# Splitting a column transform by parity: half the frequencies, sum and difference, and what moves with it

## The chip, the core and the metric

The kernel runs on one core of one Trainium2 chip. The metric is the device time of one execution in microseconds. The profile describes one execution; its span is about 2 us shorter than the device time of the same run. A run lists also the mean granted clock of TensorE, where 1 is full speed. In the profiles PE is TensorE, which does the matmuls and leaves their results in banks of a memory called PSUM; DVE is VectorE, ACT is ScalarE and POOL is GpSimd, which do the element-wise work; SPq is the queue of SyncE, which issues DMA transfers. A tile is 128 rows of the data, a period is the time from one group or tile to the next, and a releaser is the operation that ended a wait.

## The reference

The input is 2048 rows of 576 numbers in bfloat16. A layer norm, a two-dimensional real FFT, a complex weight per frequency, the inverse FFT and a residual add come first; then a second layer norm and a gated feed-forward block with a hidden width of 4608.

```python
def reference(A_x, A_w_r, A_w_i, B_x, B_w_gate, B_w_up, B_w_down):
    def _A_ref(x, w_r, w_i):
        X = rfft2(x); X = X * (w_r + 1j * w_i)
        return irfft2(X, s=(S, D)).astype(bfloat16)
    def _B_ref(x, w_gate, w_up, w_down):
        return (gelu(x @ w_gate) * (x @ w_up)) @ w_down
    h = A_x + _A_ref(_layernorm(A_x), A_w_r, A_w_i)
    return h + _B_ref(_layernorm(h), B_w_gate, B_w_up, B_w_down)     # S, D, F = 2048, 576, 4608
```

## The kernel before

All transforms are matmuls with tables. I call the stages A to D, as the prediction does.

- Stage A: statistics of the first layer norm, and the first half of the transform over rows, into `U`.
- Stage B: for each of 16 groups, the column transform (`st_D`), a small transform and the filter (`st_B`), and the way back (`st_V`). A software pipeline runs `st_D` of group i, `st_B` of i-1 and `st_V` of i-3.
- Stage C: for each of 16 tiles, the inverse column transform (`st_I`), the last small transform with the residual add (`st_N`), and for the first four tiles the second layer norm and a transpose on TensorE (`turn_pe`).
- Stage D: the feed-forward in four blocks of 512 rows. A block has 36 gate/up steps (`gu`), then the down projection. The normalized rows of the next block are transposed by DMA while the block runs.

An operation names what it reads and writes; a helper derives the semaphores.

```python
def st_D(i):                                        # stage B, column transform: 10 matmuls
    for o in range(2):                              # cosine and sine sums
        b = 2 * sl + o
        for dt in range(5):
            P.op(PE, lambda t, ...: t.matmul(bank(b, 0, 128, 0, K2), U[:, dt, g, :, :], FT[:, dt, o, 0:K2], ...))
        # o == 0: VectorE copies to CUS, o == 1: ScalarE copies to CUS
def st_B(i):
    # ... 4 matmuls, YS <- PSUM on ScalarE
    P.op(DVE, ... T1[:, sl, :, :] = YS * WS)        # 580 columns
    # ... T2 in two halves of 290, then on VectorE
    P.op(DVE, ... ZS[.., 0, ..] = T1[.., 0, :] - T1[.., 1, :])
    P.op(DVE, ... ZS[.., 1, ..] = T2[.., 0, :] + T2[.., 1, :])
def st_N(c):                                        # stage C
    for h in range(2):
        b = 4 + h                                   # the same two PSUM banks for every tile
        P.op(PE, lambda t, ...: t.matmul(bank(b, 0, 128, 0, 288), IT[:, c, :], GS[:, sl, 288*h:288*h+288], start=True, stop=True), ...)
    P.op(DVE, ... scalar_tensor_tensor(x2, banks(4, 2, 288), 1.0, x2, op0=mult, op1=add, accum_out=SB2[:, 0, c:c+1]), ...)
    P.op(ACT, ... activation(SQ, XO[:, c, :], Square, accum_out=SB2[:, 1, c:c+1]), ...)
# ... stage D
gu(0)
for tb in range(4):
    for f in range(36):
        gu(36 * tb + f + 1)                         # its first half belongs to step f + 1
        if tb == 0 and f == 20:
            ln2_a(3); ln2_b(3); ln2_c(3)
        if tb < 3 and f % 4 == 3 and f < 16:        # steps 3, 7, 11, 15
            norm(4 * (tb + 1) + f // 4)             # VectorE
            turn_dma(4 * (tb + 1) + f // 4)         # five 128x128 DMA transposes
    for p in range(4):
        down(tb, p)
```

At f = 35 the call `gu(36 * tb + 36)` already contains the first half of the next block's first step, so it needs all the transposed rows of the next block.

Of the kernel before, what the change touches and what calls it, by code (L numbers as in the profile page):

```python
# [10 lines left out]
KW = 290  # L11
ZW = 320
FF = 4608
NT = 16
# [15 lines left out]
def build_tables():  # L30
# [7 lines left out]
    T = {}  # L38
# [20 lines left out]
    T["ITAB"] = I.reshape(128, 16 * 128)  # L59

    d = np.arange(D)[:, None]
    k2 = np.arange(K2)[None, :]
    ph = 2 * np.pi * ((d * k2) % D) / D
    fd = np.zeros((640, 2, KW))
    fd[:D, 0, :K2] = np.cos(ph)
    fd[:D, 1, :K2] = np.sin(ph)
    fd[:, 0, 0] = 0.0
    T["FTAB"] = fd.reshape(5, 128, 2 * KW).transpose(1, 0, 2).reshape(128, -1)

    B = np.zeros((2, 3, 16, 4, 2, 128))  # L70
# [40 lines left out]
    T["BTAB"] = B.reshape(2, 3, 128, 128).transpose(2, 0, 1, 3).reshape(128, -1)  # L111
# [3 lines left out]
    dc = np.arange(D)[None, :]  # L115
# [6 lines left out]
    dt_ = np.zeros((5, 128, D))  # L122
    dt_[0], dt_[1] = C[0:128], N[0:128]
    dt_[2], dt_[3] = C[128:256], N[128:256]
    dt_[4, 0:33] = C[256:289]
    dt_[4, 64:96] = N[256:288]
    T["EYE"] = np.eye(128)
    T["DTAB"] = dt_.transpose(1, 0, 2).reshape(128, -1)
# [156 lines left out]
def _build(nc, A_x, A_w_r, A_w_i, B_w_gate, B_w_up, B_w_down, out):  # L285
# [34 lines left out]
    FT = sb.alloc("FT", [128, 5, 2, KW], BF16)  # L320
    BT = sb.alloc("BT", [128, 2, 3, 128], BF16)
# [13 lines left out]
    DT = sb.alloc("DT", [128, 5, D], BF16)  # L335
    IT = sb.alloc("IT", [128, NT, 128], BF16)
    GS = sb.alloc("GS", [128, 2, D], BF16)
# [22 lines left out]
    P.op(POOL, lambda g: g.memset(WS[:, :, :, K2:KW], 0.0), w=["Wz"])  # L360
    P.op(POOL, lambda g: g.memset(U[64:128, 4, :, :, :], 0.0), w=["Uz"])
    xv = A_x[0].rearrange("(p c) d -> p c d", c=NT)
    ov = out[0].rearrange("(p c) d -> p c d", c=NT)
    for i, (c0, c1) in enumerate(((0, 2), (2, 4), (4, 8), (8, 12), (12, 16))):
        P.dma(SP, XO[:, c0:c1, :], xv[:, c0:c1, :], f"x{i}", w=[("X", c) for c in range(c0, c1)])
# [5 lines left out]
    def w_loads(pl, hf, eng):  # L371
        g0, g1 = ((1, 9), (9, 16))[hf]
        src = (A_w_r, A_w_i)[pl]
        o = []
        for jj in range(4):
            o.append((WS[jj:64:4, g0:g1, pl, 0:K2], (16 * jj + g0) * K2, [[128 * K2, 16], [K2, g1 - g0], [1, K2]], jj))
            o.append((WS[64 + jj:128:4, g0:g1, pl, 0:K2], (64 + 16 * jj + 16 - g0) * K2, [[128 * K2, 16], [-K2, g1 - g0], [1, K2]], 4 + jj))
        if hf:
            for p0 in range(2):
                o.append((WS[64 * p0:64 * p0 + 64, 0, pl, 0:K2], 64 * p0 * K2, [[128 * K2, 16], [16 * K2, 4], [1, K2]], 8 + p0))  # L380
        return [lambda d=d, off=off, ap=ap, h=h: P.dma(eng, d, bass.AP(src.tensor, off, ap), f"w{pl}{hf}", r=["Wz"], w=[("W", hf, pl, h)]) for d, off, ap, h in o]

    for f in w_loads(0, 0, SP) + w_loads(0, 1, SP):
        f()
# [3 lines left out]
    P.dma(SP, IT[:, :, :].rearrange("p a b -> p (a b)"), dram["ITAB"][:, :], "it", w=["IT"])  # L388
    P.dma(SP, IDT[:, :], dram["EYE"][:, :], "eye", w=["IDT"])

    P.op(POOL, lambda g: g.memset(YS[:, :, :, K2:KW], 0.0), w=["Yz"])
    P.op(POOL, lambda g: g.memset(ZS[:, :, :, K2:ZW], 0.0), w=["Zz"])
    for f in w_loads(1, 0, POOL):
        f()
    wrest = w_loads(1, 1, POOL)


    def ln1_act(q):
        c = 4 * q + 3
        P.op(ACT, lambda a, c=c: a.activation(JNK[:, 0, :], XO[:, c, :], ACTF.Identity, accum_out=SA[:, 0, c:c + 1]),  # L400
             r=[("X", c)], w=[("SA0", c), "J0"])
        P.op(ACT, lambda a, c=c: a.activation(JNK[:, 1, :], XO[:, c, :], ACTF.Square, accum_out=SA[:, 1, c:c + 1]),  # L402
             r=[("X", c)], w=[("SA1", c), "J1"])
# [5 lines left out]
    def ln1_var(q):  # L409
        for c in range(4 * q, 4 * q + 3):  # L410
            P.op(DVE, lambda v, c=c: v.bn_aggr(MV1[:, c, :], ST1[:, c, :, :]), r=[("ST1", c, 0), ("ST1", c, 1)], w=[("MV1", c)])
        c = 4 * q + 3
        P.op(DVE, lambda v, c=c: v.scalar_tensor_tensor(TM[:, 0, c:c + 1], SA[:, 0, c:c + 1], 1.0 / (D * D), SA[:, 0, c:c + 1],
                                                        op0=ALU.mult, op1=ALU.mult), r=[("SA0", c)], w=[("TM", c)])
        P.op(DVE, lambda v, c=c: v.scalar_tensor_tensor(MV1[:, c, 1:2], SA[:, 1, c:c + 1], 1.0 / D, TM[:, 0, c:c + 1],
                                                        op0=ALU.mult, op1=ALU.subtract), r=[("SA1", c), ("TM", c)], w=[("MV1", c)])

    def ln1_sqrt(q):
        cs = slice(4 * q, 4 * q + 4)
        P.op(ACT, lambda a, cs=cs: a.activation(RS1[:, cs], MV1[:, cs, 1], ACTF.Sqrt, bias=EPT[:, 0:1]),  # L420
             r=[("MV1", c) for c in range(4 * q, 4 * q + 4)] + ["EPT"], w=[("SD1", q)])

    def ln1_scale(q, eng):
        cs = slice(4 * q, 4 * q + 4)
        P.op(DVE, lambda v, cs=cs: v.reciprocal(RS1[:, cs], RS1[:, cs]), r=[("SD1", q)], w=[("RS1", q)])
        if eng == POOL:
            P.op(POOL, lambda g, cs=cs: g.tensor_tensor(ATS[:, cs, :], ATB[:, cs, :], RS1[:, cs].unsqueeze(2).to_broadcast([128, 4, 128]), op=ALU.mult),
                 r=[("RS1", q), "ATB"], w=[("ATS", c) for c in range(4 * q, 4 * q + 4)])
        else:
            for c in range(4 * q, 4 * q + 4):  # L430
                P.op(DVE, lambda v, c=c: v.tensor_scalar(ATS[:, c, :], ATB[:, c, :], RS1[:, c:c + 1], None, op0=ALU.mult),
                     r=[("RS1", q), "ATB"], w=[("ATS", c)])
# [5 lines left out]
    def a_mm(q, dt):  # L438
        b = (5 * q + dt) % 7
        w = 128 if dt < 4 else 64  # L440
        for i in range(4):
            c = 4 * q + i
            P.op(PE, lambda t, b=b, w=w, i=i, c=c, dt=dt: t.matmul(bank(b, 0, w, 128 * i, 128 * i + 128), XO[:, c, 128 * dt:128 * dt + w],
                                                                  ATS[:, c, :], start=True, stop=True),
                 r=[("X", c), ("ATS", c)], w=[("PS", b)])

    def a_ev(q, dt, eng):
        b = (5 * q + dt) % 7
        w = 128 if dt < 4 else 64
        src = bank(b, 0, w).rearrange("p (n g e) -> p n g e", n=4, g=16)  # L450
        dst = U[0:w, dt, :, 4 * q:4 * q + 4, :].rearrange("p g n e -> p n g e")
        if eng == DVE:
            P.op(DVE, lambda v, s=src, d=dst: v.tensor_copy(d, s), r=[("PS", b)], w=[("U", q, dt)])
        else:
            P.op(ACT, lambda a, s=src, d=dst: a.activation(d, s, ACTF.Copy), r=[("PS", b)], w=[("U", q, dt)])  # L455

    P.op(ACT, lambda a: a.activation(SA[:, 0, 0:1], EPT[:, 0:1], ACTF.Sqrt), r=["EPT"], w=[("SA0", 0)])
    ln1_act(0)
    ln1_act(1)
    idle_mm(24)  # L460
    for c in range(3):
        ln1_tile(c)
    ln1_var(0)
    ln1_sqrt(0)
    ln1_act(2)
    ln1_tile(4)
    ln1_scale(0, POOL)
    for f in wrest[:4]:
        f()
    ln1_tile(5)  # L470
    ln1_tile(6)
    ln1_var(1)
    a_mm(0, 0)
    a_ev(0, 0, ACT)
    ln1_sqrt(1)
    for dt in range(1, 5):
        a_mm(0, dt)
    a_ev(0, 1, ACT)
    a_ev(0, 2, ACT)
    ln1_tile(8)  # L480
    ln1_scale(1, POOL)
    for f in wrest[4:7]:
        f()
    ln1_tile(9)
    ln1_tile(10)
    ln1_var(2)
    a_ev(0, 3, ACT)
    a_ev(0, 4, ACT)
    ln1_sqrt(2)
    ln1_act(3)  # L490
    idle_mm(4)
    for dt in range(5):
        a_mm(1, dt)
        a_ev(1, dt, ACT)
    ln1_tile(12)
    ln1_scale(2, POOL)
    for f in wrest[7:]:
        f()
    ln1_tile(13)
    ln1_tile(14)  # L500
    ln1_var(3)
    ln1_sqrt(3)
    idle_mm(4)
    for dt in range(5):
        a_mm(2, dt)
    a_ev(2, 0, ACT)
    a_ev(2, 1, DVE)
    ln1_scale(3, DVE)
    a_ev(2, 2, ACT)
    a_ev(2, 3, DVE)  # L510
    a_ev(2, 4, ACT)
    idle_mm(4)
    for dt in range(5):
        a_mm(3, dt)
        a_ev(3, dt, (ACT, DVE)[dt % 2])
    idle_mm(3)


    ukeys = [("U", q, dt) for q in range(4) for dt in range(5)] + ["Uz"]

    def st_D(i):
        g = GORD[i]
        sl = i % 2
        for o in range(2):
            b = 2 * sl + o
            for dt in range(5):
                P.op(PE, lambda t, b=b, o=o, dt=dt, g=g: t.matmul(bank(b, 0, 128, 0, K2), U[:, dt, g, :, :], FT[:, dt, o, 0:K2],  # L527
                                                                 start=(dt == 0), stop=(dt == 4)),
                     r=ukeys + ["FT"], w=[("PS", b)])
            if o == 0:  # L530
                P.op(DVE, lambda v, b=b, sl=sl: v.tensor_copy(CUS[:, sl, 0, 0:K2], bank(b, 0, 128, 0, K2)), r=[("PS", b)], w=[("CU", sl)])
            else:
                P.op(ACT, lambda a, b=b, sl=sl: a.activation(CUS[:, sl, 1, 0:K2], bank(b, 0, 128, 0, K2), ACTF.Copy), r=[("PS", b)], w=[("SU", sl)])  # L533

    def st_B(i):
# [3 lines left out]
        for b, tabs in ((4, (0, 1)), (5, (1, 2))):  # L539
            for o in range(2):  # L540
# [238 lines left out]
```

## Time and profile before

The median was 518.59 us (518.15 to 519.65, 4 runs). The profiled span was 516.4 us.

| stage | from, us | to, us | length, us |
|---|---|---|---|
| A | 0 | 21.80 | 21.8 |
| B | 21.80 | 64.16 | 42.4 |
| C | 64.16 | 89.56 | 25.4 |
| D | 89.56 | 516.4 | 426.8 |

A stage begins with its first matmul. First, from the page of the kernel before, the head of the chain that ended last: shares of the span by engine.

```profile
PE 93%; DVE 2%; ACT 2%; DMA 2%; issue 0%; SPq 0%; DVEq 0%
```

Next, the same chain in order of time. The columns are start in us, length in us, and engine, output and line. L527 is the column transform, L541 the small transform, L560 and L564 the way back; L699 is gate/up and L720 is down.

```profile
31.87 1.34 PE PS L527 x10
33.21 0.50 PE PS L541 x4
33.71 0.44 PE PS L560 x4
34.15 0.24 PE PS L564 x4
34.38 1.34 PE PS L527 x10
...
92.03 70.04 PE PS L699 x648
162.06 35.39 PE PS L720 x288
```

One group of stage B lasts 34.38 - 31.87 = 2.51 us, and all of it is TensorE. In stage D the block 0 sequence is 70.04 us of gate/up followed at once by 35.39 us of down: no wait. The 648 matmuls of this piece are 36 steps of 18, so one step takes 1.946 us.

The timeline of the kernel before in stage C (start, length, engine, line, operation, operands; in brackets the idle time before and its releaser):

```profile
68.08 0.41 PE L611 MATMUL PS<-GS,IT 128*128 128x288 bf16 x2
...
68.53 0.76 DVE L614 SCALAR_TENSOR_TENSOR XO<-PS,XO 128x576 bf16<-128x576 f32 x1 [0.70 <-PE PS L611]
...
69.55 0.41 PE L611 MATMUL PS<-GS,IT 128*128 128x288 bf16 x2
```

The residual add (L614) takes 0.76 us and reads the PSUM banks that the next tile's pair of matmuls (L611) overwrites. It is done at 69.29, before the matmuls would start at 69.55. The tile period is 1.47 us.

Last, the normalization of step 15 of block 0, in the timeline of VectorE:

```profile
123.96 0.64 DVE L640 TENSOR_SCALAR HN<-XO,TM,RS_59 128x576 bf16<-128x576 bf16 x2
```

its five transposes, in the timeline of the SyncE queue:

```profile
124.62 6.19 SPq L193 DMA_TRANSPOSE HT_84<-HN  x5
```

and the end of the traffic, in a table of windows (the length of the window, the busy time of PE, of its weight loads PEld, of DVE, ACT and POOL with counts, then the granted clock, the DMA share and GB/s):

```profile
131.75:132.00 0.25, 0.25 (x6) 0.13 (x4) 0.06 (x1) 0.05 (x1) 0.00 (x0) 1.00 0.00 0
```

The five transposes occupy the queue for 6.19 us, and the DMA engines are quiet from about 131.75. So a normalization leads to transposed rows about 7.8 us later. In this kernel nothing waits for them.

### The profile page before, as it was taken

What the parts mean: (1) busy time and instruction counts of PE and PEld (TensorE: products, weight loads), DVE (VectorE), ACT (ScalarE), POOL (GpSimd) and SP (SyncE); (2) the same over time, 40 slices, a digit from 0 to 9 for tenths busy, and PEclk for the clock granted to TensorE, in tenths of its full rate; (3) what the DMA queues carried; (4) which work ended last, traced back from release to release, by engine and by line L of the source; (5) the groups of instructions that cost most, each with busy time, mean ns of one, the idle gap of its engine ahead of it and who ended that gap; (6) DMA issues with size and microseconds to landing.
All of it is one profiled execution on the core that took longest, in us unless ns stands there. A gap on an engine that the chain in (4) does not pass through costs nothing.

```text
span 516.4 us, 10131 instructions
## 1 busy us (share of the span) xinstructions
PE 507.4 (98%) x4425; PEld 295.9 (57%) x4427; DVE 184.5 (36%) x428; ACT 152.7 (30%) x285; POOL 27.8 (5%) x48
## 2 busy tenths in 40 slices
PE   8899899999999999999999999999999999999997
PEld 3577577444445775444457754444477644444776
DVE  5687758344432112443321124433311133333111
ACT  5756677423521002332320013323200033233000
POOL 8800130000000000000000000000000000000000
PEclk9999999999999999999999999999999999999999
DMA  8999791011000000110000000100000000000000
GB/s 289 289 343 307 208 361 44 4 24 22 7 1 2 18 18 11 22 22 11 1 1 18 18 11 20 22 15 1 1 13 18 18 1 1 0 2 1 13 18 17
DMA packets 23899, 28.64 MB, mean 55 GB/s; under 512 B 11408, under 2 KB 17680, under 8 KB 23856
## 3 DMA queue, kind: packets, MB, share of 16 engines
q1 hardware_dynamic: 20560, 15.68, 10.9%
q0 software_dynamic: 3152, 11.80, 7.0%
q8 instruction: 34, 0.56, 0.5%
q10 hardware_dynamic: 144, 0.52, 0.3%
q14 instruction: 9, 0.07, 0.0%
HBM read 23.67 MB, written 2.36 MB: 50 GB/s over the span
## 4 chain that ended last, share of the span: by engine, by line
PE 93%; DVE 2%; ACT 2%; DMA 2%; issue 0%; SPq 0%; DVEq 0%
PE PS L699 55%; PE PS L720 27%; PE PS L527 4%; PE PS L602 3%; DMA XO<-in_A_x_dram 2%; PE PS L541 1%; ACT U L455 1%; PE PS L560 1%; PE PS L611 1%; PE PS L564 1%; DVE XO L614 0%; ACT JNK L400 0%; DVE ST_53 L407 0%; ACT JNK L402 0%; ACT YS L544 0%
## 5 line engine op out<-in xcount | busy, mean ns | idle before, releaser
L711 ACT ACTIVATE GL<-PS 128x512 bf16<-128x512 f32 x144 | 85.8, 597 | 293.9 <-PE PS L699 293.1
L712 DVE TENSOR_TENSOR AT<-GL,PS 128x512 bf16<-128x512 bf16 x144 | 98.9, 688 | 174.3 <-PE PS L699 169.8
L699 PE MATMUL PS<-HT_69,WGU 64*128 64x512 bf16 x1296 | 144.4, 376 | 0.0
L699 PE MATMUL PS<-HT_84,WGU 64*128 64x512 bf16 x1296 | 144.4, 376 | 0.0
L720 PE MATMUL PS<-WD,AT 128*128 128x288 bf16 x1152 | 141.8, 286 | 0.0
L720 PEld LDWEIGHTS PS<-WD,AT 128*128 128x128 bf16 x1152 | 112.4, 98 | 29.9 <-issue 1.7
L699 PEld LDWEIGHTS PS<-HT_84,WGU 64*128 64x128 bf16 x1296 | 64.5, 94 | 77.9 <-issue 0.5
L699 PEld LDWEIGHTS PS<-HT_69,WGU 64*128 64x128 bf16 x1296 | 64.5, 94 | 76.8 <-issue 0.7
L723 DVE TENSOR_TENSOR OS<-PS,XO 128x288 bf16<-128x288 f32 x32 | 14.6, 458 | 126.0 <-PE PS L720 126.0
L602 PE MATMUL PS<-DT,V 128*128 128x288 bf16 x160 | 22.1, 286 | 0.5 <-ACT V L567 0.5
L527 PE MATMUL PS<-FT,U 128*128 128x289 bf16 x160 | 22.3, 287 | 0.2 <-ACT U L455 0.2
L602 PEld LDWEIGHTS PS<-DT,V 128*128 128x128 bf16 x160 | 15.4, 98 | 4.3 <-issue 0.6
L527 PEld LDWEIGHTS PS<-FT,U 128*128 128x128 bf16 x160 | 14.5, 97 | 5.1 <-issue 0.4
L614 DVE SCALAR_TENSOR_TENSOR XO<-PS,XO 128x576 bf16<-128x576 f32 x16 | 12.1, 756 | 9.6 <-PE PS L611 9.3
L436 PE MATMUL PS<-ZD 128*128 128x512 bf16 x37 | 11.8, 475 | 1.5 <-POOL ZD L358 1.3
L617 ACT ACTIVATE SQ<-XO 128x576 bf16<-128x576 bf16 x16 | 10.9, 682 | 5.0 <-DVE XO L614 4.8
L407 DVE BATCH_NORM_STATS2 ST_53<-XO 128x6 f32<-128x288 bf16 x24 | 9.2, 443 | 5.7 <-DMA XO<-in_A_x_dram 5.7
L544 ACT ACTIVATE YS<-PS 128x578 bf16<-128x578 f32 x16 | 10.5, 655 | 1.8 <-PE PS L541 0.7
L604 ACT ACTIVATE GS<-PS 128x576 bf16<-128x576 f32 x16 | 10.2, 635 | 2.6 <-PE PS L602 2.6
L541 PE MATMUL PS<-CUS,BT 128*128 128x289 bf16 x64 | 10.6, 286 | 0.2
L533 ACT ACTIVATE CUS<-PS 128x289 bf16<-128x289 f32 x16 | 6.6, 413 | 14.0 <-PE PS L527 14.0
L546 DVE TENSOR_TENSOR T_79<-YS,WS 128x580 bf16<-128x580 bf16 x16 | 7.3, 459 | 9.1 <-ACT YS L544 9.1
(57 smaller groups left out, 173.2 us busy)
## 6 DMA issues: line engine op xcount, KB each, us to landing
WD<-in_B_w_down_dram POOLq DMA_DIRECT2D x9, 576.0 KB, 9.3
WGU<-in_B_w_gate_dram POOLq DMA_DIRECT2D x4, 1152.0 KB, 17.7
WGU<-in_B_w_up_dram SPq DMA_DIRECT2D x4, 1152.0 KB, 22.5
out_dram<-OS SPq DMA_DIRECT2D x32, 72.0 KB, 1.6
XO<-in_A_x_dram SPq DMA_DIRECT2D x3, 576.0 KB, 8.2
FT<-c_ftab SPq DMA_DIRECT2D x1, 725.0 KB, 12.7
DT<-c_dtab SPq DMA_DIRECT2D x1, 720.0 KB, 14.6
HT_84<-HN SPq DMA_TRANSPOSE x40, 2.4
```

The costliest lines, as they stand in the source:

```text
L436: P.op(PE, lambda t: t.matmul(bank(7), ZD[:, 0:128], ZD[:, :], start=True, stop=True), r=["ZD"], w=[("PS", 7)])
L527: P.op(PE, lambda t, b=b, o=o, dt=dt, g=g: t.matmul(bank(b, 0, 128, 0, K2), U[:, dt, g, :, :], FT[:, dt, o, 0:K2], start=(dt == 0), stop=( ...
L541: P.op(PE, lambda t, b=b, o=o, tb=tabs[o], sl=sl, sp_=sp_: t.matmul(bank(b, 0, 128, 0, K2), BT[:, sp_, tb, :], CUS[:, sl, o, 0:K2], start= ...
L544: P.op(ACT, lambda a, sl=sl: a.activation(YS[:, sl, :, 0:K2], banks(4, 2, K2), ACTF.Copy), r=[("PS", 4), ("PS", 5)], w=[("Y", sl)])
L602: P.op(PE, lambda t, b=b, h=h, kt=kt, c=c: t.matmul(bank(b, 0, 128, 0, 288), V[:, kt, c, :, :], DT[:, kt, 288 * h:288 * h + 288], start=(k ...
L614: P.op(DVE, lambda v, x2=x2, c=c: v.scalar_tensor_tensor(x2, banks(4, 2, 288), 1.0, x2, op0=ALU.mult, op1=ALU.add, accum_out=SB2[:, 0, c:c ...
L617: P.op(ACT, lambda a, sl=sl, c=c: a.activation(SQ[:, sl, :], XO[:, c, :], ACTF.Square, accum_out=SB2[:, 1, c:c + 1]), r=[("X", c)], w=[("S ...
L699: op = P.op(PE, lambda t, h0=h0, kt=kt, wt=wt, f=f, b=b, HT=HT, s=(half == 0 and j in (0, 5)), e=(half == 1 and j in (3, 8)): t.matmul(ban ...
L711: P.op(ACT, lambda a, s2=s2, b0=b0: a.activation(GL[:, s2, :], bank(b0), ACTF.Gelu_apprx_tanh), r=[("PS", b0)], w=[("GL", s2)])
L712: P.op(DVE, lambda v, s2=s2, b0=b0, f=f: v.tensor_tensor(AT[:, f, :], GL[:, s2, :], bank(b0 + 1), op=ALU.mult), r=[("GL", s2), ("PS", b0 + ...
L720: P.op(PE, lambda t, b=b, h=h, f=f, p=p: t.matmul(bank(b, 0, 128, 0, 288), AT[:, f, 128 * p:128 * p + 128], WD[:, f, 288 * h:288 * h + 288 ...
L723: P.op(DVE, lambda v, b=b, h=h, p=p, c=c: v.tensor_tensor(OS[:, p % 2, 288 * h:288 * h + 288], bank(b, 0, 128, 0, 288), XO[:, c, 288 * h:2 ...
```

## The change

For the cosine and sine sums over d, the frequencies k and 288-k differ only in the sign of the odd d (for the sines also in the sign of the whole, which the table of the small transform takes up). So the even and the odd d are summed for 145 frequencies, and VectorE makes the sum and the difference. That is 6 matmuls of 290 columns instead of 10 of 289 per group; the inverse likewise computes half the columns, with 6 + 4 matmuls per tile instead of 10 + 2. The small transform `st_B` gets six matmuls instead of four, with the same number of columns in all. The diff, cut to its core:

```diff
 def st_D(i):
-            for dt in range(5):
-                P.op(PE, ... matmul(bank(b, 0, 128, 0, K2), U[:, dt, g, :, :], FT[:, dt, o, 0:K2], ...))
-            # copies of the two sums, one on DVE and one on ACT
+            for dt in range(3):
+                us = (2 * o + dt) if dt < 2 else 4
+                P.op(PE, ... matmul(bank(b, 0, 128, 0, 2 * HK), U[:, us, g, :, :], FT[:, o, dt, :], ...))
+        P.op(ACT, ... ES = even sums, fp32)
+        P.op(DVE, ... CUS[.., 0:HK] = e2 + o2)
+        P.op(DVE, ... CUS[.., K2 - 1:HK - 1:-1] = e2 - o2)
 def st_B(i):
-        # T2 in two halves; both Z sums on DVE
+        P.op(DVE, ... T2[:, sl, :, :] = YS * WS[:, g, 1::-1, :])
+        P.op(POOL, ... ZS[:, z3, 0, 0:KW] = T1[:, sl, 0, :] - T1[:, sl, 1, :])
+        P.op(POOL, ... ZS[:, z3, 1, 0:KW] = T2[:, sl, 0, :] + T2[:, sl, 1, :])
 def st_N(c):
+            for i in range(2):        # 4 matmuls instead of 2, into the same banks 4 and 5
-        P.op(ACT, ... Square ...)
+        if c < 4:
+            square(c, SQ[:, sl, :], ("SQ", sl))
 # stage D
-            if tb == 0 and f == 20:
-                ln2_a(3); ln2_b(3); ln2_c(3)
-            if tb < 3 and f % 4 == 3 and f < 16:
-                norm(4 * (tb + 1) + f // 4)
-                turn_dma(4 * (tb + 1) + f // 4)
+            if tb == 0 and f < 12:
+                square(4 + f, OS[:, f % 2, :], ("OS", f % 2, 0))
+            if tb == 0 and f == 14:
+                ln2_a(1); ln2_b(1); ln2_c(1)
+            if tb < 3 and f % 4 == 3 and 16 <= f < 32:
+                norm(4 * (tb + 1) + f // 4 - 4)
+                turn_dma(4 * (tb + 1) + f // 4 - 4)
# ... also changed: stage A works in six groups (2, 2, 4, 4, 2, 2 tiles) with fewer idle matmuls,
# ... all filter loads go through the SyncE queue, and the copy of turned tiles moves from DVE to ACT
```

Three things travel with the idea. The Z sums go to GpSimd. Twelve of the sixteen squares for the second layer norm are deferred to block 0 of the feed-forward. The statistics of these twelve tiles are then ready only after step 14 of block 0, and normalization and transposes come at steps 19, 23, 27 and 31, in all blocks.

## The prediction

> **What bounds it now.** The chain of waits gives TensorE 93% of the 516.4 us span. Read in time order it has four stages. A (layer norm, first transform) ends at 21.8. B (column transform, filter, group transform) runs 21.8 to 64.2 in a steady 2.51 us per group, TensorE without a gap (1.34 column matmuls, 0.50, 0.44, 0.24). C (inverse) runs 64.2 to 89.6, 1.47 us per tile (1.23 + 0.24), dense but for the layer-norm turns. D (feed-forward) is 70.04 + 35.39 us, four times, with no gap at all.
>
> **What the change does.**
> 1. Stage B: 6 column matmuls of 290 columns for 10 of 289. At 0.134 us each that is 0.54 us less per group; TensorE's own period falls to about 2.03 (six shorter matmuls replace four, same columns). But the two Z sums move from VectorE to GpSimd. The 128x512 GpSimd multiply took 1.03-1.05 us, so 128x290 should take about 0.6 (estimate), two 1.2. The Trainium skill (SBUF — State Buffer, "Who interferes with whom") says a VectorE op with two SBUF inputs and a GpSimd op that reads SBUF exclude each other for the whole instruction. T1 and T2 are such ops (0.37 us spacing each). Serial: 0.37+0.46+1.2 plus hand-overs = about 2.15 us, more than TensorE's 2.03. So the period should be 2.15-2.25. The drain gets longer by about 0.7 us (GpSimd sums slower than VectorE's 0.22). Stage B gains about 4 us rather than the 8.6 of the matmul count.
> 2. Stage A: smaller groups, but the same bn_stats and ScalarE evictions, and the last statistics now wait on ScalarE sums in the middle. I expect 0 to 2 us longer, +0.8.
> 3. Stage C: 6+4 matmuls instead of 10+2 save 0.24 per tile by count. But the 0.76 us residual add reads the single pair of PSUM banks and has only 0.74 us of matmuls to hide behind (before 1.23). Period about 0.48+0.76+0.1 = 1.36 us, not 1.23. Gain about 2.2 us. Deferring ScalarE squares helps little there.
> 4. Stage D: the squares (0.87 us of ScalarE, twelve times) fit beside 0.60 us GELUs in a 1.946 us step, with no extra table load. But normalization and DMA transposes move from steps 3,7,11,15 to 19,23,27,31. In before, step 15's normalization began at 123.96; its five transposes occupied the queue until 130.81 and DMA activity ended about 131.8, i.e. 8.7 us after the matmuls of that step's eviction ended (123.09). In after, the first matmul of the next token block is only 3 steps = 5.84 us away. TensorE should stall about 2.9 us at the end of blocks 0, 1 and 2: +8.7 us.
>
> **Sum.** 518.5 + 0.8 - 4 - 2.2 + 8.7 = 521.8; leaning slightly to the gains, 521.0 us, range 514.5 to 527. Chances: faster by over 2% 0.05, within 2% 0.88, slower by over 2% 0.07.
>
> **What would show each step.** Stage B period 2.15-2.25 with GpSimd sums and T1/T2 not overlapping, TensorE waiting on GpSimd or ScalarE (1); 2.03 refutes the exclusion. Stage C period near 1.36, TensorE waiting on the residual add before the inverse group matmuls (3). Three TensorE gaps of about 3 us in the feed-forward, just before the block's last gate/up step, released by the transposes' DMA (4). Granted clock staying near 1.
>
> **What would make it wrong.** The transposes landing sooner, so no stall (then near 512); the exclusion weaker than stated (2 us faster) or GpSimd sums over 0.7 us (slower); filter loads, now all on one queue, landing late; the clock dropping after the 3 us gaps (slower).

## The result, and the profile after

The changed kernel took 532.04 us (median of 4 runs, 530.35 to 532.78); the ratio is 1.0252, with a 95% interval of 1.0223 to 1.0281. The change is slower by 2.5%, and the prediction of 521.0 us with a range to 527 missed it. The mean granted clock of its four runs was 0.974 to 0.987; that of the kernel before was 0.999 in its profiled run.

The profiled spans are 531.0 and 516.4 us. Where the 14.6 us lie:

| stage | before, us | after, us | measured | predicted |
|---|---|---|---|---|
| A | 21.80 | 22.94 | +1.1 | +0.8 |
| B | 42.36 | 38.27 | -4.1 | -4 |
| C | 25.40 | 26.13 | +0.7 | -2.2 |
| D | 426.84 | 443.66 | +16.8 | +8.7 |

The page of the changed kernel, head of the chain:

```profile
PE 85%; DVE 8%; issue 3%; ACT 1%; POOL 1%; DMA 1%; DVEq 0%; POOLq 0%
```

and the chain in order of time through stage D (L721 is gate/up, L742 is down):

```profile
90.05 68.10 PE PS L721 x630
158.15 3.83 issue
161.98 2.96 PE PS L721 x18
164.94 36.18 PE PS L742 x288
...
269.21 3.01 issue
272.22 3.80 PE PS L721 x18
...
379.51 3.05 issue
382.56 4.02 PE PS L721 x18
386.58 36.29 PE PS L742 x288
```

The three waits add to 9.9 us. They are labelled "issue": the profile saw no releaser for them, so the label alone does not say what was waited for. The time goes on after the waits. The 18 matmuls of the step that follows take 2.96, 3.80 and 4.02 us instead of 1.946, and two of the three down projections take 36.18 and 36.29 instead of 35.39. Together that is 4.9 + 1.7 = 6.6 us of slow matmuls. (The first wait is the longest because one of its five transposes held the queue for 2.06 us instead of 1.23; why it did stays open.) The windows around the first wait show the reason:

```profile
158.00:162.00 4.00, 0.17 (x4) 0.05 (x4) 0.69 (x1) 0.00 (x0) 0.00 (x0) 1.00 0.12 25
...
163.50:164.00 0.50, 0.50 (x6) 0.26 (x4) 0.00 (x0) 0.22 (x1) 0.00 (x0) 0.50 0.00 0
...
166.50:167.00 0.50, 0.50 (x5) 0.40 (x4) 0.00 (x0) 0.00 (x0) 0.00 (x0) 0.97 0.00 0
```

In each line the third number from the end is the granted clock. It stays at 1 through the wait and for about a microsecond after it, falls to 0.50 at 163.12, and is back at 166.53, 3.41 us later.

The timeline of stage C, to be held against that of before (L633 are the four small matmuls, L636 the residual add):

```profile
67.31 0.65 PE L633 MATMUL PS<-GS,IT 128*128 128x288 bf16 x4 [0.20 <-DVE XO L636]
...
68.00 0.76 DVE L636 SCALAR_TENSOR_TENSOR XO<-PS,XO 128x576 bf16<-128x576 f32 x1 [0.84 <-PE PS L633]
...
68.92 0.65 PE L633 MATMUL PS<-GS,IT 128*128 128x288 bf16 x4 [0.20 <-DVE XO L636]
```

The tile period is 68.92 - 67.31 = 1.61 us, longer than the 1.47 before although there are fewer matmuls. The matmuls wait 0.20 us for the residual add of the tile before.

Stage B in the timeline of TensorE:

```profile
37.05 0.92 PE L540 MATMUL PS<-FT,U 128*128 128x290 bf16 x6
37.81 0.67 PE L557 MATMUL PS<-CUS,BT 128*128 128x289 bf16 x6
38.32 0.60 PE L575 MATMUL PS<-VT,ZS 128*128 128x256 bf16 x4
38.85 0.31 PE L579 MATMUL PS<-VT,ZS 128*64 128x128 bf16 x4
39.09 0.30 PE L540 MATMUL PS<-FT,U 128*128 128x290 bf16 x1
```

One group now takes 39.09 - 37.05 = 2.04 us, without a gap on TensorE. The groups of VectorE and GpSimd operations (busy time in us, mean ns of one, then idle time before and its releaser) are, before,

```profile
L546 DVE TENSOR_TENSOR T_79<-YS,WS 128x580 bf16<-128x580 bf16 x16 | 7.3, 459 | 9.1 <-ACT YS L544 9.1
```

and after, where L562 is T1 and L565 and L566 the Z sums:

```profile
L565 POOL TENSOR_TENSOR ZS<-T_80 128x290 bf16<-128x290 bf16 x16 | 12.7, 792 | 13.4 <-DVE T_80 L562 13.0
...
L566 POOL TENSOR_TENSOR ZS<-T_81 128x290 bf16<-128x290 bf16 x16 | 11.4, 711 | 2.3
L562 DVE TENSOR_TENSOR T_80<-YS,WS 128x580 bf16<-128x580 bf16 x16 | 11.3, 704 | 1.2 <-ACT YS L560 1.1
```

T1, the same operation as before, has gone from 459 to 704 ns.

### The profile page after: what moved, and what is told of

Same layout as the page of the kernel before. It is cut to its first block, busy times and chain, and to the rows that moved or that the text cites. A ratio compares the mean times of both kernels' runs of the same rounds, so it can differ in the third digit from the quotient of the medians.

```text
span 531.0 us, 10050 instructions
## 1 busy us (share of the span) xinstructions
PE 504.2 (95%) x4346; PEld 289.1 (54%) x4347; DVE 183.7 (35%) x387; ACT 155.5 (29%) x296; POOL 43.3 (8%) x64
## 4 chain that ended last, share of the span: by engine, by line
PE 85%; DVE 8%; issue 3%; ACT 1%; POOL 1%; DMA 1%; DVEq 0%; POOLq 0%
PE PS L721 54%; PE PS L742 27%; PE PS L633 2%; DVE T_80 L562 2%; DVE XO L636 1%; PE PS L618 1%; DVE ST_53 L418 1%; DMA XO<-in_A_x_dram 1%; DVE CUS L546 1%; DVE CUS L547 1%; ACT U L476 1%; POOL ZS L566 1%; DVE V L584 1%; POOL ZS L565 1%; PE PS L540 1%
## 5 line engine op out<-in xcount | busy, mean ns | idle before, releaser
L721 PE MATMUL PS<-HT_85,WGU 64*128 64x512 bf16 x1296 | 149.0, 380 | 6.9 <-issue 6.9
L721 PE MATMUL PS<-HT_69,WGU 64*128 64x512 bf16 x1296 | 149.2, 380 | 3.0 <-issue 3.0
L742 PE MATMUL PS<-WD,AT 128*128 128x288 bf16 x1152 | 143.5, 288 | 0.0
L742 PEld LDWEIGHTS PS<-WD,AT 128*128 128x128 bf16 x1152 | 113.1, 99 | 32.0 <-issue 2.8
L721 PEld LDWEIGHTS PS<-HT_85,WGU 64*128 64x128 bf16 x1296 | 65.2, 95 | 86.3 <-issue 10.5
L721 PEld LDWEIGHTS PS<-HT_69,WGU 64*128 64x128 bf16 x1296 | 65.5, 95 | 80.5 <-issue 6.1
L745 DVE TENSOR_TENSOR OS<-PS,XO 128x288 bf16<-128x288 f32 x32 | 14.6, 457 | 127.7 <-PE PS L742 127.7
L636 DVE SCALAR_TENSOR_TENSOR XO<-PS,XO 128x576 bf16<-128x576 f32 x16 | 12.1, 757 | 14.6 <-PE PS L633 14.5
L540 PE MATMUL PS<-FT,U 128*128 128x290 bf16 x96 | 15.8, 305 | 0.9 <-DVE U L474 0.9
L618 PE MATMUL PS<-DT,V 128*128 128x289 bf16 x96 | 15.8, 306 | 0.5 <-ACT V L582 0.5
L565 POOL TENSOR_TENSOR ZS<-T_80 128x290 bf16<-128x290 bf16 x16 | 12.7, 792 | 13.4 <-DVE T_80 L562 13.0
L463 PE MATMUL PS<-ATS,XO 128*128 128x128 bf16 (+1 forms) x80 | 6.4, 222 | 6.4 <-POOL ATS L442 6.2
L633 PE MATMUL PS<-GS,IT 128*128 128x288 bf16 x64 | 10.5, 285 | 2.0 <-DVE XO L636 1.6
L620 ACT ACTIVATE GS<-PS 128x578 bf16<-128x578 f32 x16 | 10.4, 648 | 5.5 <-PE PS L618 5.3
L557 PE MATMUL PS<-CUS,BT 128*128 128x289 bf16 (+2 forms) x96 | 11.2, 254 | 0.6 <-ACT ES L543 0.4
L562 DVE TENSOR_TENSOR T_80<-YS,WS 128x580 bf16<-128x580 bf16 x16 | 11.3, 704 | 1.2 <-ACT YS L560 1.1
L618 PEld LDWEIGHTS PS<-DT,V 128*128 128x128 bf16 x96 | 9.7, 103 | 3.6 <-issue 0.6
L566 POOL TENSOR_TENSOR ZS<-T_81 128x290 bf16<-128x290 bf16 x16 | 11.4, 711 | 2.3
L575 PE MATMUL PS<-VT,ZS 128*128 128x256 bf16 x64 | 9.6, 272 | 2.1 <-POOL ZS L566 2.1
```

Source lines behind the costliest of these rows:

```text
L540: P.op(PE, lambda t, b=b, o=o, dt=dt, us=us, g=g: t.matmul(bank(b, 0, 128, 0, 2 * HK), U[:, us, g, :, :], FT[:, o, dt, :], start=(dt == 0) ...
L562: P.op(DVE, lambda v, g=g, sl=sl: v.tensor_tensor(T1[:, sl, :, :], YS[:, sl, :, :], WS[:, g, :, :], op=ALU.mult), r=[("Y", sl)] + wk, w=[( ...
L565: P.op(POOL, lambda v, sl=sl, z3=z3: v.tensor_tensor(ZS[:, z3, 0, 0:KW], T1[:, sl, 0, :], T1[:, sl, 1, :], op=ALU.subtract), r=[("T1", sl) ...
L566: P.op(POOL, lambda v, sl=sl, z3=z3: v.tensor_tensor(ZS[:, z3, 1, 0:KW], T2[:, sl, 0, :], T2[:, sl, 1, :], op=ALU.add), r=[("T2", sl)], w= ...
L618: P.op(PE, lambda t, b=b, h=h, i=i, kt=kt, c=c: t.matmul(bank(b, 0, 128, 0, K2), V[:, kt, c, :, :], DT[:, 3 * h + i, 0:K2], start=(i == 0) ...
L633: P.op(PE, lambda t, b=b, h=h, i=i, c=c, rhs=rhs: t.matmul(bank(b, 0, 128, 0, 288), IT[:, h * i, c, :], rhs, start=(i == 0), stop=(i == 1) ...
```

## The experiments

My theory after reading the result had two parts. The late transposes alone make the waits of stage D; and the waits lower TensorE's clock, which costs another 6.6 us. The rivals were that the deferred squares are to blame, and that the clock falls for some other reason. Eleven kernels ran. Those of one group ran on one chip, with its own runs of the kernel before. e1 and e7 are the changed kernel with one edit, and e3 is the kernel before with one. All others contain the edit of e2 as well; only what they add is shown.

| run | median, us | ratio to before (95%) | mean clock, profiled run | B, us | C, us | D, us |
|---|---|---|---|---|---|---|
| changed kernel | 532.04 | 1.0252 (1.0223-1.0281) | 0.981 | 38.3 | 26.1 | 443.7 |
| e1_dense_gap | 526.19 | 1.0133 (1.0103-1.0163) | 0.993 | 37.6 | 25.7 | 438.3 |
| e2_early | 516.02 | 0.9935 (0.9907-0.9963) | 0.989 | 38.4 | 25.7 | 427.1 |
| e3_before_late | 531.24 | 1.0230 (1.0192-1.0268) | 0.996 | 42.4 | 25.4 | 438.7 |
| e4_early_nbuf | 514.84 | 0.9914 (0.9889-0.9939) | 0.990 | 37.2 | 25.2 | 427.1 |
| e5_z_dve | 515.98 | 0.9943 (0.9919-0.9966) | 0.997 | 37.9 | 26.4 | 427.1 |
| e6_warm | 513.96 | 0.9906 (0.9883-0.9929) | 1.000 | 37.1 | 25.0 | 427.1 |
| e7_step18 | 519.91 | 1.0016 (0.9988-1.0044) | 0.997 | 37.1 | 25.0 | 431.6 |
| e8_squares_in_c | 515.46 | 0.9936 (0.9900-0.9972) | 0.990 | 37.3 | 26.7 | 427.1 |
| e9_z_split | 513.70 | 0.9903 (0.9873-0.9933) | 1.000 | 35.9 | 25.0 | 427.1 |
| e10_turn_later | 513.17 | 0.9888 (0.9863-0.9913) | 0.990 | 37.4 | 23.8 | 427.1 |
| e11_all | 511.43 | 0.9856 (0.9832-0.9881) | 1.000 | 36.7 | 23.0 | 427.1 |

All outputs were correct. The kernel before had medians of 519.38 (e1 to e4), 518.35 (e5 to e8) and 518.71 us (e9 to e11).

### e1_dense_gap: the same waits, with TensorE kept busy

```diff
+            if f == 35 and tb < 3:
+                for _ in range((17, 14, 14)[tb]):     # useless, into a free PSUM bank
+                    P.op(PE, lambda t, tb=tb: t.matmul(bank(7), WGU[:, 0, 0:128], HTS[tb % 2][:, 0, :], ...), w=[("PS", 7)])
             gu(36 * tb + f + 1)
```

> The changed kernel, with 17, 14 and 14 useless 512-column matmuls put into a free PSUM bank just before the first step of blocks 1, 2 and 3, where TensorE waits 3.8, 3.0 and 3.1 us. Theory (idleness lowers the clock): the useless work takes what was idle time, about 3 us each, the wait itself costs the same, but the granted clock stays at 1 and the 6.6 us of slow matmuls after the three waits vanish: about 525.5 us. Rival (the clock falls for another reason, such as load): the clock still falls to about 0.5 after the waits and the time stays near 532 us.

Measured: 526.19 us, 5.9 us below the changed kernel; its slowest run (527.59) lies below the fastest of the changed kernel (530.35). In the windows of this run, of which the first covers the end of block 0's steps and the useless matmuls, and the others the first step of the next block and the down projection:

```profile
157.00:161.00 4.00, 3.87 (x20) 1.69 (x22) 0.69 (x1) 0.00 (x0) 0.00 (x0) 1.00 0.08 16
161.00:163.00 2.00, 2.00 (x21) 0.81 (x18) 0.09 (x1) 0.60 (x1) 0.00 (x0) 1.00 0.00 0
163.00:165.00 2.00, 2.00 (x19) 1.61 (x17) 0.60 (x1) 0.00 (x0) 0.00 (x0) 1.00 0.00 0
```

The clock stays at 1.00 after all three waits, and the first steps take 2.05, 2.05 and 2.12 us. The waiting itself is still there (stage D 438.3 us). So it is the idleness of TensorE in these waits that lowers the clock after them.

### e2_early: normalization and transposes back to an earlier place

```diff
-            if tb < 3 and f % 4 == 3 and 16 <= f < 32:
-                norm(4 * (tb + 1) + f // 4 - 4)
-                turn_dma(4 * (tb + 1) + f // 4 - 4)
+            f0 = 15 if tb == 0 else 3
+            if tb < 3 and f % 4 == 3 and f0 <= f < f0 + 16:
+                norm(4 * (tb + 1) + (f - f0) // 4)
+                turn_dma(4 * (tb + 1) + (f - f0) // 4)
```

> The changed kernel with normalization and transposes moved back: steps 15, 19, 23, 27 in block 0 (after the deferred statistics at step 14) and steps 3, 7, 11, 15 in blocks 1 and 2. Theory (the late transposes alone make the feed-forward longer): no wait of TensorE in the feed-forward, granted clock 1 there, the whole 16.5 us back: about 515.5 us, 3 us below the kernel before. Rival (the twelve deferred squares on ScalarE, or the extra matmuls elsewhere, share the blame): a gain of less than 14 us.

Measured: 516.02 us, as the theory had it. The chain of this run in stage D:

```profile
89.82 70.04 PE PS L721 x648
159.86 35.38 PE PS L742 x288
```

There is no wait, and stage D is back at 427.1 us. The twelve deferred squares are still in block 0 of this kernel, so they cost TensorE nothing there.

### e3_before_late: only the late place, in the kernel before

```diff
-            if tb < 3 and f % 4 == 3 and f < 16:
-                norm(4 * (tb + 1) + f // 4)
-                turn_dma(4 * (tb + 1) + f // 4)
+            if tb < 3 and f % 4 == 3 and 16 <= f < 32:
+                norm(4 * (tb + 1) + f // 4 - 4)
+                turn_dma(4 * (tb + 1) + f // 4 - 4)
```

> The kernel before with only normalization and transposes moved to steps 19, 23, 27, 31 of each block, as the change has it; nothing else of the change. Theory: three waits of about 3 us with the clock falling to half after each, together 15 to 17 us: about 534.5 us. Rival (the waits need the deferred squares or the new DMA order as well): under 525 us.

Measured: 531.24 us (529.59 to 533.17). The place alone costs 2.3%, nearly as much as the whole change. The size was below the expected 534.5, and the chain of the profiled run shows why (L699 is gate/up):

```profile
160.17 2.98 issue
163.15 3.60 PE PS L699 x18
...
270.22 3.82 issue
274.04 2.12 PE PS L699 x18
...
379.64 3.04 issue
382.68 2.12 PE PS L699 x18
```

All three waits are there, with 9.8 us in all, but only the first was followed by a slow step. The mean clock of the four runs went from 0.996 to 0.987, and the slower runs are those with the lower clock. A wait of 3 to 4 us thus lowers the clock often but not always. It is not the length alone: the second wait, 3.82 us, did not, and the first, 2.98 us, did. What decided is worked out in the section on why the prediction was wrong.

### e7_step18: one step earlier

```diff
-            if tb < 3 and f % 4 == 3 and 16 <= f < 32:
+            if tb < 3 and f % 4 == 2 and 16 <= f < 32:
```

> The changed kernel with normalization and transposes just one step (1.95 us) earlier, steps 18, 22, 26, 30. Theory: the waits shrink by 1.95 us each, from 3.8, 3.0, 3.1 to about 1.9, 1.1, 1.1 us, 4.1 us in all, and gaps this short leave the clock at 1: early transposes plus 4.1, about 520 us, a gain of 12 us although only 5.9 us of waiting went. If the clock falls after such short gaps too, 523 to 526 us.

Measured: 519.91 us (518.35 to 520.41). The waits in the profiled run added to 3.9 us, the longest being 1.7, and the clock was 1.00 after each. So 1.95 us less of waiting per block gained 12 us. The profiled run was the fastest of the four; the others were 1.4 to 2.1 us slower, with mean clocks of 0.987 to 0.990, and no trace says where their clock fell.

### e4_early_nbuf: a second pair of banks in stage C

```diff
-            b = 4 + h
+            b = (4 if c % 2 == 0 else 6) + h      # and the residual add reads the same pair
```

> As the run with early transposes, and the inverse group matmuls of odd tiles go to PSUM banks 6 and 7 instead of 4 and 5, so that a tile no longer waits for the residual add of the tile before it. Theory (that single pair of banks makes the 1.60 us period of the inverse stage): period about 1.25 us, stage from 26.2 to about 22.5 us, time about 3.5 us below the run with early transposes, so about 512 us. Rival (ScalarE's evictions or VectorE's own work set the period): under 1 us gained.

Measured: 514.84 us, 1.2 us below the run with early transposes, where 3.5 was expected. The timeline of TensorE in this run:

```profile
64.36 0.65 PE L633 MATMUL PS<-GS,IT 128*128 128x288 bf16 x4
...
65.99 0.67 PE L633 MATMUL PS<-GS,IT 128*128 128x288 bf16 x4 [0.22 <-ACT GS L620]
...
67.24 0.66 PE L633 MATMUL PS<-GS,IT 128*128 128x288 bf16 x4
```

The period is now 1.63 and 1.25 us in turn, and the longer one waits for ScalarE's copy. Stage C is 0.5 us shorter than in the run with early transposes; of the 1.5 us between the two profiled spans 1.1 lie in stage B, which this edit does not touch and which began at a slow clock in the other run. The single pair of banks was a limit, and ScalarE with its copy and its square came right behind it, with VectorE's normalization in the tiles with turns. The theory held for the first limit and was wrong about the gain.

### e8_squares_in_c: what the deferral was worth

```diff
-        if c < 4:
+        if True:                                     # all sixteen squares stay in stage C
             square(c, SQ[:, sl, :], ("SQ", sl))
-            if tb == 0 and f < 12:
-                square(4 + f, OS[:, f % 2, :], ("OS", f % 2, 0))
```

> The run with early transposes, but all sixteen squares stay in the inverse stage behind their residual add, none in the feed-forward. Theory (the period of 1.60 us per tile comes from residual add and matmuls in turn, and ScalarE with 0.65 + 0.87 us fits beside it, so deferring the squares bought nothing): the inverse stage within 0.5 us for tiles without turns, about 1 us longer in all because of the four tiles where ScalarE also copies the turned tile, so 516 to 517.5 us. Rival (deferral was worth its place): 3 us or more slower, 519 us.

Measured: 515.46 us, with runs from 514.70 to 517.07 that follow the clock (1.000 to 0.987). The median shows no loss against the run with early transposes, but its scatter is larger than the 1 us expected. Like clocks say more: the run at a clock of 1.000 took 514.70, against 513.9 to 514.0 with the squares deferred in e6_warm below, and stage C, 26.7 us, is the longest of all runs, in part for a slow clock at its start. An estimate from these figures is that the deferral was worth about 0.7 us, far less than the waits cost.

### e5_z_dve and e9_z_split: the Z sums

```diff
-        P.op(POOL, ... ZS[:, z3, 0, 0:KW] ...)       # e5 and e9: this one on DVE
-        P.op(POOL, ... ZS[:, z3, 1, 0:KW] ...)       # e5 only: this one as well
+        P.op(DVE, ...)
```

> The run with early transposes, and the two sums that make Z are put back on VectorE. Theory (GpSimd's sums and VectorE's two-input products exclude each other, which stretches T1 from 460 to about 700 ns but fits in TensorE's period): T1 and T2 are back at about 460 ns, VectorE now has about 2.13 us of work per group (0.74 + 0.74 + 0.44 + 0.21), so the period goes from 2.03 to about 2.13, and the tail of the stage gets about 1.5 us shorter because VectorE's sums take 0.22 us each: together about 516 us, no change. Rival (the stretch of T1 has nothing to do with GpSimd): T1 stays at about 700 ns. If GpSimd was a net loss: 514 us or less.

Measured: 515.98 us. The group of T1 in this run:

```profile
L562 DVE TENSOR_TENSOR T<-YS,WS 128x580 bf16<-128x580 bf16 x16 | 7.3, 454 | 1.4 <-ACT YS L560 1.1 <-DMA WS<-in_A_w_i_dram 0.4
```

T1 is back at 454 ns, so its stretch came from GpSimd. The period was 2.11 us with VectorE busy all the time, and the tail of the stage was shorter. The median shows no net change, as expected, but this flatters the edit: where stage B began at full clock, as it did here (37.9 us), it took 37.1 with the sums on GpSimd (e6 and e7); in the run with early transposes it began slow.

> The run with early transposes; of the two Z sums the first goes back to VectorE, right behind T1 and T2, the second stays on GpSimd, where it can run beside the PSUM operations of VectorE. Theory (the 2.03 us period of stage B is the closed loop of operations that exclude each other: T1 0.31 after GpSimd's end, T2 0.38, first sum 0.53, 0.14 between, second sum 0.67; TensorE's own work is 0.76+0.51+0.44+0.24 = 1.95): period 1.95 us and a tail about 0.7 us shorter, together about 2 us less, 514 us. Rival (TensorE sets 2.03 us): period stays 2.03, time 515.3 us.

Measured: 513.70 us (512.72 to 515.18). The time was near the theory's figure, but the theory was wrong. The timeline of TensorE in this run:

```profile
37.79 0.92 PE L540 MATMUL PS<-FT,U 128*128 128x290 bf16 x6
...
39.83 0.92 PE L540 MATMUL PS<-FT,U 128*128 128x290 bf16 x6
```

The period is 39.83 - 37.79 = 2.04 us, as with both sums on GpSimd, while T1 had fallen to 461 ns. TensorE sets it: 0.76 + 0.51 + 0.53 + 0.24 us between the starts of its four groups. The gain lies in the tail, where stage B is 1.2 us shorter than in the other runs with a warm start (35.9 against 37.1), and in the clock, which was 1.000 in the profiled run.

### e6_warm: useless matmuls in the gaps of stages A and B

```diff
-    idle_mm(16)                                       # and 2, 2, 2, 1 before the groups of stage A
+    idle_mm(24)                                       # and 3, 10, 10, 5, and 4 at the end
+        if i >= NG + 1:                               # tail of stage B, banks 0 and 2 are free
+            for _ in range(7): P.op(PE, ... matmul(bank(0, 0, 128, 0, 2 * HK), BT[:, 0, 0, :], FT[:, 0, 0, :], ...))
+        # and 4 more, into bank 2, after the last group
```

> The run with early transposes, with more useless matmuls in the gaps of stage A and in the tail of stage B, so that TensorE hardly idles before the first matmuls of stages B and C. Theory (the gaps there also lower the clock: 12 matmuls at the start of B took 2.8 us and at the start of C 2.4 to 3.1 us, against 1.6 us at full clock): both first dozens back at about 1.6 us, mean granted clock above 0.995, 2 to 3 us less than with early transposes, about 513.5 us. Rival (those first matmuls are slow for another reason, such as the new operand layout): no gain, 516 us, or a loss if the useless matmuls delay useful ones.

Measured: 513.96 us, with all four runs between 513.89 and 513.99 and a clock of 1.000 in each. The first dozen matmuls took 1.66 us in stage B and 1.66 in stage C by the timeline, against 2.80 and 2.42 in the run with early transposes. So the gaps in stages A and B lowered the clock too. Without them the scatter of the runs is gone as well (0.1 us).

### e10_turn_later and e11_all: what is left

```diff
-            b = 4 + h
+            b = (6 if c % 2 == 0 else 4) + h
-        if c in (7, 9, 11, 13):
-            turn_pe((c - 7) // 2)
+        if c in (8, 10, 12, 14):
+            turn_pe((c - 8) // 2)
```

> The run with early transposes and two pairs of banks for the inverse group matmuls (even tiles 6 and 7, odd tiles 4 and 5), and the four turns of normalized tiles come one tile later, so that TensorE does not wait for the normalization. Theory (with two pairs of banks the remaining loss sits in the tiles with turns, 3.33 us for two tiles against 2.77 of matmuls): 2.2 us below the run with two pairs of banks alone, about 512.6 us. Rival (ScalarE's copies set the pace there too): less than 0.8 us gained.

Measured: 513.17 us, 1.7 us below the run with two pairs of banks alone. Stage C is 23.8 us. Nearer to the theory than to the rival. Two things changed at once, the turns and the order of the bank pairs, and no run separates them.

> Everything together on the changed kernel: early transposes, useless matmuls in the gaps of stages A and B, two pairs of banks and later turns in the inverse stage, the first Z sum on VectorE. If the gains add: 516.0 - 2.1 (clock) - 1.2 - 2.2 (inverse stage) - 2 (stage B) = 508.5 us, about 2% below the kernel before; granted clock above 0.995. If they overlap: 510 to 512 us.

Measured: 511.43 us (511.23 to 511.56), ratio 0.9856 (0.9832 to 0.9881). This version beats both kernels: by 7 us the kernel before, by 20.6 us the changed one. The gains overlapped, as the second branch of the expectation said. One overlap can be seen: the useless matmuls in the tail of stage B are in the way now that the tail is shorter (36.7 us against 35.9 in the run with split sums).

## Why the prediction was wrong

**Stage D, the step that failed.** The prediction had the mechanism of the waits right, and nearly the size: "TensorE should stall about 2.9 us at the end of blocks 0, 1 and 2: +8.7 us"; measured 3.83, 3.01 and 3.05, or 9.9. What failed is the line "Granted clock staying near 1". It named the other case only as a risk. In the profiled run the clock fell to half at each wait, twice for 3.41 us and the third time for 6.83, and the slow matmuls cost 6.6 us. Some 0.3 to 0.5 of this is not the clock: the first step after a wait takes 2.05 to 2.12 us instead of 1.946 at full clock too. The run with useless matmuls shows it directly, and the move in the kernel before shows that the place alone is enough.

The page "TensorE: Matmul & The Clock Gate" of the Trainium skill, in its Part 1, gives the two clock states, says that full speed is lost after an idle window of about 3.4 us, and that the window runs free of the program; its closing table asks for no idle gaps over about 3 us. The predicted 2.9 us lies just below both figures. The runs say that three microseconds are inside the doubtful range: all three waits of the changed kernel's profiled run lowered the clock, one of three did in the kernel before with late transposes, and none of three did when the longest was 1.7 us.

The window itself can be seen in the traces, which record when the granted clock changed. The five falls during the changed kernel's work begin at 23.17, 60.72, 163.12, 272.35 and 381.57 us, and each distance between two of them is a whole number of 3.413 us (11, 30, 32 and 32); the same holds within every other run with more than one fall. Cut the span into these windows, and the spread of the waits is no chance. First a window of the changed kernel that ended in a fall, at the third wait, and the moment after its end; then the two windows that share the 3.82 us wait of e3, where the clock stayed up (after the length, the first number is the busy time of TensorE):

```profile
378.16:381.57 3.41, 1.35 (x14) 0.39 (x8) 0.92 (x2) 0.60 (x1) 0.00 (x0) 1.00 0.14 29
381.58:381.66 0.08, 0.00 (x0) 0.00 (x0) 0.00 (x0) 0.00 (x0) 0.00 (x0) 0.50 0.00 0
```

```profile
268.58:272.00 3.42, 1.64 (x16) 0.56 (x12) 1.22 (x2) 0.60 (x1) 0.00 (x0) 1.00 0.10 19
272.00:275.41 3.41, 1.37 (x14) 0.78 (x16) 0.00 (x0) 0.23 (x1) 0.00 (x0) 1.00 0.05 10
```

The nine waits of the three profiled runs fall apart in the same way: the clock fell at the end of a window in which TensorE had idled for 2.06, 2.27, 2.60 or 3.01 us, and at the end of none with 2.05 or less. The ends of matmuls are modelled, so the border is less sharp than these figures look. So in this stage a wait costs clock if more than about 2.05 us of it lie in one window. An estimate from that: a wait below 2.05 us never does, one above 4.1 always, and between them it depends on where the window happens to end. This is read off the traces; no run moved a wait against the window to test it. It does not carry over to stages A and B, where the clock fell after windows with as little as 1.3 us of idle time.

**Stage C, mis-sized.** The prediction's term was "Period about 0.48+0.76+0.1 = 1.36 us" with a "Gain about 2.2 us". The loop is as it was described, matmuls and residual add in turn. It measured 0.65 from the first start to the last end of the four matmuls, 0.04 to the add, 0.76 for it and 0.16 until the matmuls start again: 1.61 us. I had counted the four matmuls by their spacing (0.48) and left out how long the last one takes to come through (0.17), and allowed 0.1 for hand-overs that measured 0.20. Where the clock stayed up, stage C took 25.0 us against the 23.2 predicted (25.4 - 2.2); the slow clock at its start added 1.1 us in the profiled run of the changed kernel.

**Stage B, right in the sum by luck, not in the terms.** -4.1 us against -4. "the period should be 2.15-2.25" was wrong: it is 2.04. VectorE and GpSimd do exclude each other, as "SBUF — State Buffer", section "Who interferes with whom", of the Trainium skill states: T1 takes 704 ns beside GpSimd's sums and 454 without. But "2.03 refutes the exclusion" was a bad test. The stretch fits into TensorE's own 2.04 us, if only just (in the trace the loop of the operations that exclude each other takes 2.03), and taking it away (split sums) left the period as it was. What ate the rest of the gain was fill and tail, 37.1 - 16 x 2.04 = 4.5 us against 42.4 - 16 x 2.51 = 2.2 before, and a slow clock at the start that cost about 1.1 us. I had allowed 0.7 for the tail and nothing for the clock.

**Stage A** was +1.1 against +0.8; nothing was tested there. That the gaps between its groups lower the clock at the start of stage B was not foreseen.

**The cause of the slowdown** is thus not the parity split. With the late place undone, the changed kernel is 0.65% faster than the one before, and with the other limits taken away 1.4%. The halved column transform saves about 0.47 us per group, which is what TensorE's period shows. How much of the remaining 1.1 us in stage A is due to the new groups there stays open.

## What to carry to other kernels

When work is moved later, count back from its first reader: here a normalization and its five DMA transposes needed 7.8 us in the kernel before and 8.9 at the end of block 0 of the changed one (from 153.06 to 161.98; 8.1 in the two blocks after it), and had 5.1 (from 153.06 to 158.15, where TensorE began to wait). Where TensorE sets the time, a wait of 3 us may cost more than its length (here 9.9 us of waits cost another 6.6), because the clock can fall after it; useless work in the gap shows how much is which. When a stage loses matmuls, look at what had been hiding behind them: a loop through one PSUM bank pair can make it slower than before.

## What the Trainium skill lacked or had wrong

- "TensorE: Matmul & The Clock Gate", Part 1 and the closing table: the free-running window of about 3.4 us agrees with the traces (3.413 us). But the page ties the loss of full speed to an idle window and to gaps over about 3 us. In stage D a window in which TensorE was still busy for 1.35 of 3.41 us was enough, and the length of the gap did not decide: waits of 3.0 to 3.8 us lowered the clock in four of six cases in two profiled runs, and the 3.82 us wait that two windows shared did not. The clock fell between 1.0 us before and 1.1 us after work had begun again. It stayed at 0.50 for 3.41 us in three cases, and for 6.83 in the one where the wait took 0.99 us of the first slow window as well.
- The same page tells of short idle gaps in close succession only for the cycling through PSUM banks, and gives no measure for them. In stage A of the changed kernel no wait was longer than 1.8 us, but TensorE was busy for only 1.7 of the 4 us from 16 to 20 and 2.1 of the 3.41 before the fall at 23.17, and the clock at the start of stage B was 0.54. Filling the gaps brought it to 1.00.
- "SBUF — State Buffer", "Who interferes with whom": agrees (704 against 454 ns). Whether the blocking costs anything, each case has to show: here the period was 2.04 us with and without it.
- "GPSIMD Engine Reference", "Performance versus the Vector engine": about 2.6 cycles per element at 1.2 GHz, measured there in fp32, gives an estimate of 628 ns for 290 elements; a sum in bfloat16 beside which T1 was not stretched (split sums) measured 671 ns.
- No page that I read gives the time from a normalization to rows transposed by DMA. Here one 128x128 transpose occupied the issuing queue for 1.23 us and landed 2.4 us after its issue (medians), and five of them were done 7.8 us (kernel before) and 8.9 us (changed kernel) after the normalization began.
